# Twelve tiles' queries of a linear-attention layer, projected at the ends of the recurrent layers

## The chip, the cores and the metric

The kernel runs on one core of one Trainium2 chip. The metric is the device time of one execution, in microseconds (us).

## The reference

Four layers work in turn on x, 2048 rows of 512 bf16 numbers: a recurrent memory layer A, a linear-attention layer B, then A and B again with the same weights. Each adds its result to its input.

```python
def _B_ref(x, wqkv, wo):                       # 32 heads of 16
    qkv = (x @ wqkv).reshape(B, S, 3, H, Dh).transpose(2, 0, 3, 1, 4)
    q, k, v = qkv[0], qkv[1], qkv[2]
    phi = lambda t: jnp.where(t > 0, t + 1, jnp.exp(t)) + 1e-06
    pq, pk = phi(q), phi(k)
    kv = jnp.einsum('bhsd,bhse->bhde', pk, v)  # over all rows
    z = jnp.einsum('bhsd->bhd', pk)            # over all rows
    num = jnp.einsum('bhqd,bhde->bhqe', pq, kv)
    den = jnp.einsum('bhqd,bhd->bhq', pq, z)[..., None] + 1e-06
    return (num / den).transpose(0, 2, 1, 3).reshape(B, S, D) @ wo

x = A_x
x = x + _A_ref(_layernorm(x), mem0, Wq, Wk, Wv, Wo, seg_len)
x = x + _B_ref(_layernorm(x), wqkv, wo)
x = x + _A_ref(_layernorm(x), mem0, Wq, Wk, Wv, Wo, seg_len)
x = x + _B_ref(_layernorm(x), wqkv, wo)
```

`_A_ref` goes through 64 segments of 32 rows in order. In each, 8 memory rows and the segment's 32 rows are projected to queries, keys and values of 32 heads of 128, attend to each other under a mask, and go through Wo. The first 8 output rows are the next segment's memory, so the segments form a recurrence; the other 32 are the layer's output.

Layer B needs the sums kv and z over all rows before any output. Its queries are needed only then.

## The kernel before, in words

**Tiles and layers.** The rows form 16 tiles of 128 (four segments each). The program has two passes, called layers 0 and 1 here, each made of an A and a B. `a_layer` walks over the 64 segments s: keys and queries (`kq0`, `kq1`), values (`v`), memory attention (`mem0`, `mem1`), output projection (`out`), the next memory (`next`), the attention of the segment's own rows (`x`), and the residual (`res`). All weights of A stay in SBUF.

**The linear layer inside the recurrent one.** When a tile's four segments are done, `residual` brings their rows from `y_sb` into `dx_sb` with small DMAs, half of them from POOL's queue and half from SP's, and adds them to the tile in `x_sb` (line 2421). Then `b_in` (step `bi`) runs for the tile: layernorm (line 2058 begins it), a transposing DMA to `xlnT`, and the projection by `wqkv_sb` to keys, values and queries. Here `rows` issues, for each of four chunks of the contraction, four matmuls for the keys (line 2516) and, with the same stationary operand, four each for values and queries (line 2010). `phi` is one exponential on ACT (2489) and two DVE operations (2490, 2491). Keys and values are added to kv and z (lines 2547, 2549). The finished queries go to `pq_scratch` in DRAM and the rows of x to `xs_scratch`.

**The end of a layer.** The last tile cannot be hidden: its last segment's output, the residual, the layernorm (transposed on TensorE here, line 2075), projection, kv and z, then `b_mid` (`bm`), which folds kv and wo into one matrix `MB_sb`, follow each other. Only then can `b_out` produce a tile's output. Of layer 0, `b_out` of tiles 0 and 1 stands in this end (`bo`), because layer 1's first segments need them; the other tiles' follow in layer 1, one tile every four segments, each reading x and queries back from DRAM. Of layer 1, `b_out` of all 16 tiles (`bl`) runs at the very end, from queries and rows that `last_rows` loads four tiles at a time into the room of Wq and Wk.

**Fillers.** `spin` multiplies the constant `one_sb` with itself into a bank that nobody reads. `SPIN` lists six: one at the start of the program (`(0, 4)`), four at the end of layer 0 (`(0, 0)`, `(0, 2)`, `(0, 3)`, `(1, 1)`) and one at the end of layer 1 (`(1, 0)`).

**Order.** Every operation has a key (layer, step, name, number). The table `PLACE` gives each a due time and, for some, the engine (`a` for ACT, `v` for DVE). `schedule` sorts all operations by it, so each engine's order, DMA queues included, is written out by hand; each engine then runs its list strictly in that order and waits on semaphores. PSUM banks are given out in the same order. The due times set the order alone, nothing starts or waits by the clock.

## Time and profile before

| | us |
|---|---|
| three runs: median (lowest to highest) | 1599.27 (1597.75 to 1600.19) |
| profiled execution, own time | 1588.73 |
| its span, first to last instruction | 1586.8 |
| TensorE busy | 1522.3 (96%) |
| VectorE busy | 1218.4 (77%) |
| ScalarE busy | 986.6 (62%) |

The profile is of one execution. PE is TensorE's matmuls, PEld its weight loads, which overlap them, DVE is VectorE, ACT ScalarE, POOL GpSimd, SP the engine that only issues DMAs. A matmul's busy time includes its drain, so that consecutive ones overlap; how long one takes in a row is read from the distance of the starts. In rows of stretches the columns are the stretch, its length, busy time and count of each engine, the granted TensorE clock, the busy share of the DMA engines, and GB/s. Layer 0 ends and layer 1 begins at about 770 to 791 us; layer 1's end begins at about 1549 us.

### The profile page before, as it was taken

The page shows a single profiled execution, that of the slowest core. Times are in us where ns is not written, and L with a number is a line of the kernel's source. Part 1 is how long each engine was busy: PE and PEld are TensorE (multiplying, and loading weights), DVE is VectorE, ACT ScalarE, POOL GpSimd, SP SyncE. Part 2 cuts the span into 40 slices and gives each one's busy share as a digit, 9 for nine tenths or more (in the row PEclk, how much of TensorE's full clock was granted, in tenths as well). Part 3 has the DMA queues.
Part 4 walks back from the last instruction along what each step waited for, and adds up shares of the span by engine and source line. Part 5 has one row for each costly group of instructions (what it writes and reads, how often), then busy time and mean ns, then how long its engine had stood idle before and what let it go on. Part 6 is the DMA issues. An engine that isn't in the chain of part 4 may idle for free.

```text
span 1586.8 us, 97637 instructions
## 1 busy us (share of the span) xinstructions
PE 1522.3 (96%) x48853; PEld 820.6 (52%) x40499; DVE 1218.4 (77%) x3496; ACT 986.6 (62%) x3075; POOL 191.6 (12%) x388
## 2 busy tenths in 40 slices
PE   6999999999999999999899999999999999999997
PEld 1455555555555555555445555545555555555453
DVE  2678878877777888777688787778787778787877
ACT  2566575666666666666366666656666666666555
POOL 2011111011111101111101111011110111110110
PEclk9999999999999999999999999999999999999999
DMA  9300000001010001101000100110101110000115
GB/s 381 115 23 21 20 22 15 20 23 24 23 20 20 18 22 20 27 17 24 25 8 17 27 25 19 27 26 17 30 14 26 27 24 24 24 18 25 31 33 146
DMA packets 79347, 58.13 MB, mean 37 GB/s; under 512 B 58872, under 2 KB 73624, under 8 KB 77400
## 3 DMA queue, kind: packets, MB, share of 16 engines
q1 hardware_dynamic: 65912, 36.30, 8.7%
q0 software_dynamic: 12864, 15.46, 3.4%
q8 instruction: 350, 5.73, 1.5%
q14 instruction: 61, 0.50, 0.1%
q10 hardware_dynamic: 160, 0.14, 0.0%
HBM read 25.57 MB, written 10.35 MB: 23 GB/s over the span
## 4 chain that ended last, share of the span: by engine, by line
PE 82%; DVE 7%; ACT 5%; SPq 3%; DMA 3%; issue 1%; DVEq 0%
PE pb L2121 29%; PE pb L2010 21%; PE pb L2350 18%; PE pb L2022 8%; SPq L1924 2%; DMA dx_sb<-y_sb 2%; ACT arena_sb L1893 2%; PE pb L2516 2%; PE pb L2212 1%; PE pb L2289 1%; DVE arena_sb L1894 1%; DVE arena_sb L2141 1%; PE pb L2377 1%; DVE st_sb L2058 1%; DVE y_sb L2360 1%
## 5 line engine op out<-in xcount | busy, mean ns | idle before, releaser
L1893 ACT ACTIVATE arena_sb<-pb 128x512 bf16<-128x512 f32 (+5 forms) x1205 | 529.5, 475 | 310.9 <-PE pb L2010 174.7
L2121 PE MATMUL pb<-Wk_sb,arena_sb 128*32 128x512 bf16 x4096 | 362.6, 380 | 2.5 <-ACT arena_sb L1893 2.2
L1894 DVE CAST arena_sb<-pb 128x512 bf16<-128x512 f32 (+4 forms) x570 | 296.9, 529 | 76.8 <-PE pb L2010 46.5
L2350 PE MATMUL pb<-Wo_sb,arena_sb 128*32 128x256 bf16 x10368 | 337.6, 273 | 6.9 <-issue 2.4
L2141 DVE STREAM_TRANSPOSE arena_sb<-arena_sb 128x256 f32<-128x256 f32 x640 | 263.7, 431 | 62.0 <-ACT arena_sb L1893 55.0
L2350 PEld LDWEIGHTS pb<-Wo_sb,arena_sb 128*32 128x32 bf16 x10368 | 258.6, 96 | 48.7 <-DVE arena_sb L2260 12.5
L2022 PE MATMUL pb<-arena_sb 128*32 128x128 bf16 (+2 forms) x10800 | 270.7, 208 | 7.8 <-DVE arena_sb L1894 2.7
L2121 PE MATMUL pb<-Wq_sb,arena_sb 128*32 128x512 bf16 x3072 | 265.5, 379 | 1.1 <-ACT arena_sb L1893 0.7
L1909 POOL DMA_DIRECT2D dx_sb<-y_sb x252 | 128.2, 512 | 1135.0 <-DVE y_sb L2360 608.2
L2022 PEld LDWEIGHTS pb<-arena_sb 128*32 128x32 bf16 x10800 | 190.9, 96 | 133.6 <-issue 33.7
L2121 PE MATMUL pb<-Wv_sb,arena_sb 128*32 128x512 bf16 x2560 | 252.3, 379 | 1.3 <-DMA Wv_sb<-in_A_Wv_dram 0.9
L2010 PE MATMUL pb<-Wv_sb,arena_sb 128*32 128x512 bf16 x2560 | 252.8, 379 | 0.0
L2121 PEld LDWEIGHTS pb<-Wk_sb,arena_sb 128*32 128x32 bf16 x4096 | 109.8, 97 | 191.9 <-issue 104.4
L2010 PE MATMUL pb<-Wq_sb,arena_sb 128*32 128x512 bf16 x2048 | 200.6, 379 | 0.0
L2121 PEld LDWEIGHTS pb<-Wq_sb,arena_sb 128*32 128x32 bf16 x3072 | 84.9, 96 | 99.0 <-issue 47.1
L1893 ACT ACTIVATE outW_sb<-pb 64x256 f32<-64x256 f32 x138 | 52.2, 378 | 107.4 <-PE pb L2350 88.4
L2360 DVE TENSOR_TENSOR y_sb<-pb,outW_sb 64x256 bf16<-64x256 f32 x162 | 68.7, 424 | 57.6 <-ACT outW_sb L1893 53.7
L2260 DVE TENSOR_TENSOR arena_sb<-pb,arena_sb 128x128 bf16<-128x128 f32 x252 | 73.0, 290 | 46.6 <-PE pb L2022 16.5
L2300 DVE TENSOR_TENSOR arena_sb<-arena_sb,bo_sb 128x512 bf16<-128x512 bf16 x256 | 103.2, 417 | 2.6
L2010 PE MATMUL pb<-Wk_sb,arena_sb 128*32 128x512 bf16 x1024 | 102.1, 379 | 0.0
L2121 PEld LDWEIGHTS pb<-Wv_sb,arena_sb 128*32 128x32 bf16 x2560 | 71.0, 96 | 60.1 <-issue 34.4
L2231 ACT ACTIVATE arena_sb<-pb 128x160 bf16<-128x160 f32 x256 | 78.0, 306 | 18.9 <-PE pb L2212 11.1
(111 smaller groups left out, 1805.0 us busy)
## 6 DMA issues: line engine op xcount, KB each, us to landing
Wk_sb<-in_A_Wk_dram SPq DMA_DIRECT2D x1, 4096.0 KB, 13.7
Wq_sb<-in_A_Wq_dram SPq DMA_DIRECT2D x1, 4096.0 KB, 24.5
Wv_sb<-in_A_Wv_dram SPq DMA_DIRECT2D x1, 4096.0 KB, 34.1
Wo_sb<-in_A_Wo_dram SPq DMA_DIRECT2D x16, 256.0 KB, 7.4
xs_scratch<-x_sb POOLq DMA_DIRECT2D x32, 128.0 KB, 2.0
pq_scratch<-arena_sb POOLq DMA_DIRECT2D x31, 128.0 KB, 2.3
x_sb<-xs_scratch POOLq DMA_DIRECT2D x16, 128.0 KB, 2.5
dx_sb<-y_sb SPq DMA_DIRECT2D x126, 12.0 KB
```

The source lines that it names most:

```text
L1893: return e.activation(o() if callable(o) else o, i() if callable(i) else i, ACTF.Copy)
L1894: return e.tensor_copy(o() if callable(o) else o, i() if callable(i) else i)
L1909: add(eng, lambda e: e.dma_start(o, i), 0.55 if eng == "pool" else 0.66, reads=reads, writes=writes, dsem="%s%d" % (kind, k), lat=lat + (0 ...
L2010: return pe.add_instruction(mybir.InstMatmult(name=nc.get_next_instruction_name(), engine=mybir.EngineType.PE, ins=[pe.lower_ap(x), pe.low ...
L2022: r = pe.matmul(o[q], w[:, q], x, start=start, stop=stop, skip_group_check=True, tile_position=(0, 32 * j))
L2121: r = pe.matmul(o, blk[:, c, :], w, start=(c == 0), stop=(c == 3), tile_position=(0, 32 * j))
L2141: add("dve", lambda v: v.transpose(dst, src(img[:, k, :].bitcast(F32))), 0.445, reads=[("img", k, h) for h in range(2)], writes=[dkey])
L2231: add("act", lambda a: a.activation(PQ[:, r2, b, 64:224], tl.f32()[:, 64:224], ACTF.Exp, scale=SCALE), c_act(160), tiles=[tl], writes=[("P ...
L2260: add("dve", lambda v: v.tensor_tensor(oTb[:, s % NO, 16 * b:16 * b + 16, 0:8].rearrange("p (i j) q -> p j i q", i=4), heads(pv.f32()[:, 0 ...
L2300: add("dve", lambda v, b=b: v.tensor_tensor(Pbx[:, :, b, :].rearrange("p j (k x) -> p j k x", k=4), px[:, b, :].rearrange("p (k x) -> p k ...
L2350: r = pe.matmul(tl.f32()[32 * j:32 * j + 32, 0:256], oT[:, 4 * hh + n, :], Wo_sb[:, 8 * n + hh, 256 * d:256 * d + 256], start=(hh == 0 and ...
L2360: add("dve", lambda e: e.tensor_tensor(y_sb[0:64, k, :], tl.f32()[a, 0:256], outW[c, v, :], ALU.add), c_dve(256), reads=[("outW", w)], til ...
```

## The change

For eight tiles of layer 0 (`LATE[0]`: 8 to 13, 6 and 7) and four of layer 1 (4 to 7), `b_in` projects keys and values alone and writes the normalised rows (`xln2`) to a new DRAM scratch, `xn_scratch`, in place of the queries.

- `late_queries`, after layer 0's segments: four transposing DMAs on SP's queue bring two tiles each into buffers of layer 0 that are no longer read (`vleft[:, 0]`, `oTl[:, 0]`, `vimg[:, 0]`, `kT`). Each tile is projected, goes through `phi` and to `pq_scratch`, as before.
- `last_queries`, at the end of layer 1: one of the four loads of queries becomes a load of normalised rows of tiles 4 to 7 into the room of Wk (`XN`); their queries are projected, already transposed, straight into `XQ`.
- Five of the six fillers are removed; the one at the start of the program stays.
- The whole table `PLACE` is new, so the order of all operations changes.

```diff
+    xn_view = nc.dram_tensor("xn_scratch", [S, D], BF16, kind="Internal").ap().rearrange("(t p) d -> t p d", p=128)
-    SPIN = {(0, 0): (24, 256, 72), (1, 0): (12,), (1, 1): (22, 256, 84), (0, 2): (5,), (0, 3): (7,), (0, 4): (30, 512, 10)}
+    SPIN = {(0, 4): (30, 512, 10)}
+    LATE = {0: (8, 9, 10, 11, 12, 13, 6, 7), 1: (4, 5, 6, 7)}
...
+    def late_queries():
+        flat = lambda v: v.rearrange("p (c t x) -> p c t x", c=4, t=2)
+        rooms = [(flat(vleft[:, 0].rearrange("p b g d -> p (b g d)")), [("vl", 0, 0), ("vl", 0, 1)]),
+                 (flat(oTl[:, 0].rearrange("p n x -> p (n x)")), [("oTl", 0, 0), ("oTl", 0, 1)]),
+                 (flat(vimg[:, 0]), [("v", 0, 0), ("v", 0, 1)]),
+                 (flat(kT.rearrange("p h j x e -> p (h j x e)")), [("kT", 0), ("kT", 1)]),
+                 (flat(vimg[:, 1]), [("v", 1, 0), ("v", 1, 1)])]
+        late_t = LATE[0]
+        for (room, keys), n in zip(rooms, range(0, len(late_t), 2)):
+            t0 = late_t[n]
+            P.at(0, n, "lx")
+            add("sp", lambda e, room=room, t0=t0: e.dma_start_transpose(
+                room.rearrange("p c t x -> p c (t x)"), xn_view[t0:t0 + 2].rearrange("t p d -> (t p) d")), 1.8,
+                reads=[("xn", t0), ("xn", t0 + 1)], writes=keys, dsem="dlx%d" % n, lat=4.4)
+            for i in range(2):
+                P.at(0, n + i, "lq")
+                e, k, tq = room[:, :, i, :], ("lq", n + i), P.tile()
+                rows_of(e, keys, (0, tq))
+                phi(tq, e, k)
+                x_move(quarters(pq_view[t0 + i]), e, n + i, keys + [k], [("pq", t0 + i)], "dlq")
+
+    def last_queries():
+        for i in LATE[1][::4]:
+            for fc in range(4):
+                P.at(1, i + fc, "lq")
+                tq = P.tile()
+                for c in range(4):
+                    add("pe", lambda pe, c=c, fc=fc, i=i, tq=tq: tiled(
+                        pe, tq.f32()[:, :], wqkv_sb[:, c, 128 * fc:128 * fc + 128], XN(i)[:, c, :], c == 0, c == 3),
+                        c_pe(1, 512), reads=["wqkv", ("RE", i), ("RE", i + 1)], tiles=[tq])
+                phi(tq, XQ[:, fc, i:i + 4, :].rearrange("p t x -> p (t x)"), ("XQ", i, fc), P.res["Wq"][1])
...
     def b_in(layer, step, t):
-        if end:
+        if end or late_q:
             rows((D, tk), (2 * D, tv))
         else:
             rows((D, tk), (2 * D, tv), (0, tq))
...
+        if late_q:
+            P.count = 22
+            x_move(xn_view[t], xln2[:, ln, :], t % 4, [("xln", ln)], [("xn", t)], "dxn")
+            return
...
     def last_rows(step):
+                if not w and i in LATE[1]:
+                    nd = add("sp", lambda e, i=i: e.dma_start_transpose(XN(i), xn_view[i:i + 4].rearrange("t p d -> (t p) d")), 2.6,
+                             reads=[("xn", t) for t in range(i, i + 4)], writes=[("RE", i), ("RE", i + 1)], after=P.res["Wk"][1],
+                             dsem="dlxn%d" % i, lat=4.8)
...
     load_wo_b(1)
     a_layer(0)
+    late_queries()
     b_mid(0, NSEG + 2)
...
     last_rows(NSEG)
+    last_queries()
     b_mid(1, NSEG + 2)
```

`rows_of` is the former inner function `rows` of `b_in` with the stationary rows as an argument. The projection of a late tile loads its stationary operand by itself, where before the queries used the one that the keys had loaded.

## The prediction

> **What bounds the kernel now.** I read the page first, then four long stretches of the span, then TensorE's order of time through the end of the first layer, then the chain of waits there, and last the one place where the clock falls.

> ```profile
> span 1586.8 us, 97637 instructions
> PE 1522.3 (96%) x48853; PEld 820.6 (52%) x40499; DVE 1218.4 (77%) x3496; ACT 986.6 (62%) x3075; POOL 191.6 (12%) x388
> ```

> TensorE (PE) is busy 96% of the span. The stretches, with PE, weight loads, VectorE (DVE), ScalarE (ACT) and POOL in us, say where the rest lies:

> ```profile
> 40.00:766.00 726.00, 712.08 (x23108) 387.14 (x19156) 566.69 (x1663) 460.79 (x1456) 87.16 (x167) 1.00 0.11 26
> 766.00:791.00 25.00, 19.94 (x608) 11.46 (x528) 16.76 (x41) 8.41 (x20) 3.69 (x7) 1.00 0.09 26
> 791.00:1530.00 739.00, 720.73 (x23332) 391.62 (x19360) 580.47 (x1667) 475.71 (x1501) 86.01 (x165) 1.00 0.10 23
> 1530.00:1587.00 57.00, 45.71 (x1396) 24.84 (x1240) 42.88 (x95) 32.34 (x70) 3.67 (x7) 1.00 0.44 115
> ```

> Inside the layers PE is busy 712.08 of 726 us (98.1%) and 720.73 of 739 us (97.5%), while DVE stands near 78%. A matmul taken out there shortens the run by nearly its slot. At the ends of the layers it is different: from 766 to 791 us PE has 5.06 us idle, and part of what counts as busy is filler, the rows that write a tile from the constant `one_sb` at lines 2037 and 2010:

> ```profile
> 771.89 0.40 PE L2022 MATMUL pb<-y_sb,selz_sb 128*32 128x256 bf16 x8 [0.98 <-DVE y_sb L2360]
> 772.12 2.25 PE L2037 MATMUL pb<-one_sb 128*32 128x256 bf16 x76
> 774.19 0.72 PE L2010 MATMUL pb<-one_sb 128*32 128x256 bf16 x20
> 776.15 0.41 PE L2075 MATMUL pb<-id_sb,arena_sb 128*32 128x128 bf16 x16 [1.24 <-DVE arena_sb L2064]
> 777.09 0.40 PE L2516 MATMUL pb<-arena_sb 128*32 128x512 bf16 x4 [0.53 <-DVE arena_sb L1894]
> ...
> 778.83 0.39 PE L2516 MATMUL pb<-arena_sb 128*32 128x512 bf16 x4
> 780.75 0.24 PE L2539 MATMUL pb<-arena_sb,one_sb 128*32 128x128 bf16 x4 [1.53 <-DVE arena_sb L2491]
> ...
> 781.68 0.40 PE L2037 MATMUL pb<-one_sb 128*32 128x512 bf16 x4
> 781.89 1.04 PE L2010 MATMUL pb<-one_sb 128*32 128x512 bf16 x16
> ...
> 784.21 0.39 PE L2037 MATMUL pb<-one_sb 128*32 128x512 bf16 x4
> 784.42 1.47 PE L2010 MATMUL pb<-one_sb 128*32 128x512 bf16 x24
> 785.72 1.46 PE L2022 MATMUL pb<-arena_sb 128*32 128x128 bf16 x32
> 787.00 2.58 PE L2037 MATMUL pb<-one_sb 128*32 128x256 bf16 x88
> 789.49 0.61 PE L2022 MATMUL pb<-arena_sb 128*32 128x512 bf16 x8
> 790.69 0.83 PE L2121 MATMUL pb<-Wq_sb,arena_sb 128*32 128x512 bf16 x12
> ```

> From first start to the next work the four fillers take about 2.6 us (772.12 on), 1.1 (781.68 to 782.75), 1.5 (784.21 to 785.72) and 2.5 (787.00 to 789.49): 7.7 us. With the 5.06 us idle, some 12.7 us of PE are free in this end. What sets its length is a chain that goes through DVE, ACT and one DMA:

> ```profile
> 768.72 0.43 SPq L1909
> 769.19 3.64 DMA dx_sb<-y_sb
> 772.93 0.43 DVE x_sb L2421
> ```

> **What is taken out of the layers.** A tile's query projection is four groups of four matmuls with 512 columns. Eight such groups start between 777.09 and 778.83 us, so one takes 1.74 / 8 = 0.2175 us and a tile 0.87 us. Eight tiles of layer 0 and four of layer 1 make 7.0 + 3.5 = 10.4 us. Since 2% of these stretches is PE waiting for others, and these waits need not shrink, I take off a tenth, 1.0 us (bounds 0 and 2). That leaves 9.4 us. The queries' ACT and DVE work also leaves; these engines have slack there, so that gains nothing by itself. On POOL the write of the normalised rows takes the place of the write of the finished queries, 128 KB each, in each of the twelve tiles; the eight writes of layer 0's late queries come later, behind the chain.

> **What is added at the end of layer 0.** 7.0 us of matmuls against 12.7 us free: by capacity they fit. The changed order puts a first tile's groups into the last segments and 52 query matmuls (13 groups, 2.8 us) between the row pick and the layernorm's turns, where the first filler and its idle time filled 772.12 to 776.15. I cost them on PE at nothing; without that cover they would cost up to 7.0 us. Each tile brings one exponential on ACT and two operations on DVE:

> ```profile
> L2491 DVE SCALAR_TENSOR_TENSOR arena_sb<-pb,arena_sb 128x512 bf16<-128x512 f32 x64 | 43.2, 680 | 0.8
> L2489 ACT ACTIVATE arena_sb<-pb 128x512 bf16<-128x512 f32 x64 | 36.6, 593 | 21.3 <-PE pb L2010 18.3 <-PE pb L2022 1.9 <-PE pb L2532 1.1
> L2490 DVE TENSOR_SCALAR arena_sb<-arena_sb 128x512 bf16<-128x512 bf16 x64 | 18.1, 284 | 14.7 <-ACT arena_sb L2489 14.2
> ```

> DVE gets 8 x (0.680 + 0.284) = 7.7 us where it has 25 - 16.76 = 8.2 us free, and the chain runs through DVE. A chain step that arrives behind a 0.68 us operation waits for it. Against that, 3.64 us of the chain is a DMA, during which DVE has little else to do, and a late query may spill into the next layer's first segments, since its tile is read much later. Bounds 0 and 7.7 us; I take 1.5, nearer the low end because ACT has over 16 us free and DVE's free time just holds the work.

> **The end of layer 1.** The four tiles' matmuls (3.5 us) replace this filler, 2.6 us long:

> ```profile
> 1551.95 0.39 PE L2037 MATMUL pb<-one_sb 128*32 128x512 bf16 x4
> 1552.17 2.54 PE L2010 MATMUL pb<-one_sb 128*32 128x512 bf16 x44
> ```

> Their 4 x 0.964 = 3.9 us on DVE meet 57 - 42.88 = 14.1 us free, but behind 1562 us that engine is nearly full. Bounds 0 and 3.9 us; I take 0.7.

> **The added transposing loads.** Layer 0's end gets four loads of two tiles on SP's queue, and one of layer 1's four loads takes normalised rows in place of queries.

> ```profile
> L2049 SPq DMA_TRANSPOSE arena_sb<-pq_scratch x16: 1197/1200/2328, 714.3 to 1445.3; - x16
> L2618 SPq DMA_TRANSPOSE Wq_sb<-pq_scratch x4: 1757/1956/2857, 1540.7 to 1554.0; - x4
> arena_sb<-pq_scratch SPq DMA_TRANSPOSE x16, 2.8
> Wq_sb<-pq_scratch SPq DMA_TRANSPOSE x4, 4.7
> ```

> A load of one tile holds the queue 1.20 us and lands in 2.8, of four tiles 1.96 and 4.7; one of two tiles I estimate at 1.45 and 3.4 us. In the changed order three of them stand directly ahead of the layer's last moves of `dx_sb`, the DMA of the chain above. Two wait for TensorE's last reads of a value buffer and of the keys, so the moves are queued behind these waits, and the DVE addition of line 2421 behind the moves. Bounds: 0, and 3 x 1.45 = 4.4 us. I take 0.4, since the last rows are written after the keys' last use, and the loads should be issued by then.

> **The fillers' clock.** Without fillers PE is less dense, and this kernel shows what that can do:

> ```profile
> 1044.70:1048.10 3.40, 0.83 (x24) 0.33 (x16) 1.56 (x5) 0.22 (x2) 0.56 (x1) 1.00 0.00 0
> 1048.00:1050.00 2.00, 1.45 (x35) 0.46 (x30) 2.00 (x7) 1.31 (x6) 0.00 (x0) 0.54 0.18 66
> 1050.00:1052.00 2.00, 1.72 (x68) 1.10 (x57) 1.11 (x4) 1.32 (x6) 0.00 (x0) 0.61 0.63 127
> 1559.80:1563.20 3.40, 1.48 (x60) 0.99 (x64) 3.11 (x11) 1.52 (x3) 0.00 (x0) 1.00 1.06 346
> PE pb L2220 <- DVE arena_sb L2141: 4.3, 4, 3.0
> 1042.92 0.52 POOL L1909 DMA_DIRECT2D dx_sb<-y_sb  x1 [2.85 <-DVE st_sb L2059]
> DVE x_sb L2421 <- DMA dx_sb<-y_sb: 13.2, 16, 3.4
> ```

> After 3.40 us with 0.83 us of work (24%) the granted clock fell to 0.54 and 0.61; with 1.48 us (44%) it stayed at 1.00. If the third and fourth filler of layer 0 went and nothing took their place, the 3.4 us before 789.49 would hold the work of 786.1 to 787.0, 0.9 us (26%), which is close to the first. A fall costs about half of 3.4 us, 1.7. Bounds 0 and 1.7; I take 0.5. [...]

> **The stall at 1046 us.** The same rows show a loss that the change does not aim at. A move of `dx_sb` from POOL started only at 1042.92, after 2.85 us, DVE stood 3.4 us at line 2421, PE 3.0 us, and then the clock fell for about 3.4 us: 3.0 us and at least 1 us in slower matmuls, some 4 us. It hangs on what DVE runs between the row sum and line 2421, and the whole order is made anew, so it may vanish (4.0 us gained), stay or come up elsewhere (0). One bad case in about 31 such places here says that one such stall is as likely as none: I take half, 2.0. [...]

> **The sum.** -10.4 + 1.0 + 1.5 + 0.7 + 0.4 + 0.5 = -6.3, and -2.0 for the stall: -8.3 us. The profiled execution took 1588.73 us (span 1586.8), so it would be 1580.4. The runs' median is 1599.27, 10.5 us above it; nothing in the trace says where these lie, so I carry the difference over unchanged: 1599.3 - 8.3 = 1591.0 us.

> **The rivals.** (a) DVE becomes the bound of the ends. Its place is 769 to 791 and 1550 to 1562 us, its price all of the 7.7 + 3.9 = 11.6 us on the chain, with the clock and SP at 1.7 and 0.4: -9.4 + 11.6 + 2.1 = +4.3, 1603.6 us. It ends slower once more than 7.3 of the 11.6 us land on the chain. For it: the chain there is DVE's. Against: 8.2 and 14.1 us free, and spilling is allowed. (b) The stall stays and the new order adds one more of 4 us: -6.3 + 4.0 = -2.3, 1597.0 us. For it: 16 waits at line 2421 show how tight these moves are; against: 15 of them sum to 9.8 us. (c) The move does not shorten the layers: each segment's memory feeds the next, and if that recurrence were the bound, the removed groups would turn into waits: 0 + 1.5 + 0.7 - 2.0, about 1599.5 us. PE's 98% speaks against it.

> **How the numbers follow.** The forecast gets 0.72, (a) 0.10, (b) 0.12, (c) 0.06. The forecast's own range is 1587.0 (stall gone, ends 2 us less than taken) to 1595.0 (stall kept, 2 us more on the ends). To hold 8 in 10 the whole range takes in (b) and the edge of (c): 1586.5 to 1599.5. Faster by over 0.2% (3.2 us, about what a measurement of this kernel can tell from no change): 0.72 and a part of (b), 0.77. Within: the rest of (b) and (c), 0.13. Slower: (a), 0.10.

> **What would show it.** Right: the last layernorm of layer 0 (line 2058's counterpart, 774.17 us before) some 6 us earlier, the first key products of layer 1 (790.69) 4 to 6 us earlier, no rows on `one_sb` at these ends, query groups in their place, PE still at 98% inside. Wrong: PE waiting in the ends for DVE in pieces of 0.7 us; a PE wait for `xn_scratch`; a long wait at line 2421; a clock below 1.00 near 790 us.

## The result, and the profile after

| | us |
|---|---|
| changed kernel, median of 9 runs (lowest to highest) | 1591.70 (1586.66 to 1594.18) |
| kernel before on the same chip, 9 runs | 1597.77 (1594.76 to 1601.56) |
| ratio, 95% interval | 0.9955 [0.994, 0.997] |
| profiled execution after, own time / span | 1591.70 / 1589.9 |

Faster by 0.45%, some 7 us (4.8 to 9.6). The forecast was 1591.0. In these and the later sets the kernel before had medians of 1594.9 to 1597.8, under the 1599.27 of the three runs that the prediction started from: the time came out right, the gain was forecast a little too large. The changed kernel was timed in one set alone. Four later kernels that differ from it by small edits (a_nodve, a_fill, a_act, a_fill_act, below) were 2.4 to 5.7 us under the kernel before of their own sets, so the 7 us may be on the high side. The first lines of the page after, and four stretches of it (stretch, length, PE, weight loads, DVE, ACT and POOL busy, granted clock, DMA share, GB/s):

```profile
span 1589.9 us, 97342 instructions
PE 1517.8 (95%) x48573; PEld 822.2 (52%) x40515; DVE 1222.8 (77%) x3529; ACT 985.0 (62%) x3042; POOL 198.1 (12%) x396
```

```profile
40.00:766.00 726.00, 707.28 (x22988) 386.83 (x19160) 559.33 (x1638) 459.71 (x1456) 87.43 (x167) 1.00 0.12 27
766.00:792.00 26.00, 20.08 (x500) 10.33 (x472) 21.93 (x55) 13.54 (x29) 7.51 (x12) 0.91 0.29 50
792.00:1530.00 738.00, 716.96 (x23176) 391.64 (x19272) 581.94 (x1695) 465.95 (x1452) 87.84 (x168) 1.00 0.11 23
1530.00:1590.00 60.00, 50.20 (x1504) 27.95 (x1380) 46.82 (x107) 36.80 (x79) 4.22 (x8) 0.99 0.46 114
```

PE is still at 97% inside the layers. At the end of layer 0 DVE went from 16.76 of 25 us to 21.93 of 26, and the granted clock from 1.00 to 0.91. TensorE's order of time there (start, duration, operation, and the idle time before it with what ended it):

```profile
772.43 0.40 PE L2034 MATMUL pb<-y_sb,selz_sb 128*32 128x256 bf16 x8 [0.63 <-DVE y_sb L2373]
772.66 2.98 PE L2519 MATMUL pb<-arena_sb 128*32 128x512 bf16 x52
775.59 0.41 PE L2088 MATMUL pb<-id_sb,arena_sb 128*32 128x128 bf16 x16
...
785.16 1.49 PE L2034 MATMUL pb<-arena_sb 128*32 128x128 bf16 x32 [1.74 <-DMA arena_sb<-pq_scratch]
789.28 1.05 PE L2034 MATMUL pb<-arena_sb 128*32 128x512 bf16 x8 [2.64 <-DVE arena_sb L2723]
790.11 0.65 PE L2088 MATMUL pb<-id_sb,arena_sb 128*32 128x128 bf16 x16
790.54 1.07 PE L2034 MATMUL pb<-arena_sb 128*32 128x512 bf16 x8
791.39 1.93 PE L2134 MATMUL pb<-Wq_sb,arena_sb 128*32 128x512 bf16 x16
```

The 52 query matmuls stand where the first filler stood and take 2.98 us, about the 2.8 that the prediction gave them. The other two gaps are bare now: 1.74 us for the transposing load of tile 1's queries, 2.64 us for DVE. Behind them the sixteen matmuls of `Wq_sb` take 1.71 us to the next start at 793.10, 0.107 us each, twice the 0.2175 / 4 of the prediction: the granted clock is 0.50. Four stretches around it:

```profile
783.70:787.10 3.40, 1.45 (x32) 0.59 (x32) 2.66 (x8) 2.58 (x5) 0.00 (x0) 1.00 0.08 20
787.10:790.50 3.40, 1.22 (x24) 0.66 (x28) 3.31 (x8) 1.19 (x4) 0.00 (x0) 0.50 0.00 0
790.50:793.90 3.40, 3.40 (x44) 0.97 (x28) 1.95 (x4) 0.42 (x2) 1.51 (x2) 0.50 0.54 111
794.00:798.00 4.00, 4.00 (x80) 0.97 (x40) 2.31 (x6) 1.56 (x5) 0.50 (x1) 1.00 0.08 4
```

**A yardstick for all runs.** In the table below, the first matmul of each "next memory" (line 2377 before, 2390 after) cuts the span: layer 0 runs from that of segment 0 to that of segment 62, its end from there to segment 0 of layer 1, and so on. The columns of waits need a word. One of the page's DMA queues has about one packet for every 256 instructions of TensorE, and I take it to bring TensorE's program in pieces:

```profile
q8 instruction: 350, 5.73, 1.5%
```

350 packets of 16,384 bytes for 89,788 instructions of TensorE recorded in before (matmuls, weight loads and 436 that only wait): about 256 instructions a piece. In dense stretches, above all in the output products (line 2350 before, 2363 after), TensorE halts without any wait that the profile knows ("issue"), and in all fourteen profiles each such halt stands at one place modulo 256 of its instruction stream (193 or 194, counted from the first recorded instruction). I call that place a boundary. After a boundary the next packet starts a median of about 1 us later, and where TensorE halts at the following boundary it goes on a median of 2.5 to 2.6 us after that packet's start. "Waits" sums, over all boundaries, the longest distance of two starts next to the boundary less 0.10 us, where it is over 0.22 us; w0 and w1 are the parts of it in layers 0 and 1.

```
kernel         layer 0     w0  end 0  layer 1     w1  end 1     span  waits  span-waits
before           708.6    2.3   48.8    730.4    2.8   49.6   1586.8    5.5      1581.3
b_again          713.2    3.4   47.7    735.5    6.3   49.6   1595.3   10.1      1585.2
b_pad            720.9   11.1   47.3    745.1   18.0   50.5   1613.2   29.2      1584.0
b_nospin         713.9    4.3   51.2    741.3   13.8   51.8   1607.7   19.0      1588.7
b_noq            714.5    8.3   47.8    735.0   11.0   51.1   1597.9   21.1      1576.8
b_thin           710.2    4.8   47.9    727.3    4.3   51.5   1586.3    9.5      1576.8
b_thin_nophi     711.2    4.3   47.7    727.4    6.1   50.3   1586.1   10.8      1575.3
after            708.8    5.4   50.0    731.4    3.9   50.4   1589.9   10.2      1579.7
a_nodve          706.0    7.7   49.3    733.5    6.5   52.4   1590.8   14.9      1575.9
a_fill           710.4    8.6   47.9    732.3    5.2   50.1   1590.0   14.6      1575.4
a_act            707.4    7.6   50.2    732.2    4.6   51.5   1590.8   12.9      1577.9
a_fill_act       706.2    6.0   47.8    734.3    4.4   51.1   1588.8   10.7      1578.1
a_pad            721.2   20.9   50.3    743.9   17.6   53.1   1618.0   41.0      1577.0
a_wide           714.6   10.5   50.7    740.6   14.4   51.9   1607.2   27.2      1580.0
```

Each line is one profile. Two of the same kernel (before, b_again) differ by 8.5 us in the span and by 3.9 us less the waits; smaller differences of single profiles are not read.

### The profile page after: what moved, and what is told of

Same layout as the page of the kernel before. It is cut to its first block, busy times and chain, and to the rows that moved or that the text cites. A ratio compares the mean times of both kernels' runs of the same rounds, so it can differ in the third digit from the quotient of the medians.

```text
span 1589.9 us, 97342 instructions
## 1 busy us (share of the span) xinstructions
PE 1517.8 (95%) x48573; PEld 822.2 (52%) x40515; DVE 1222.8 (77%) x3529; ACT 985.0 (62%) x3042; POOL 198.1 (12%) x396
## 4 chain that ended last, share of the span: by engine, by line
PE 80%; DVE 7%; ACT 4%; DMA 3%; SPq 3%; issue 1%; POOL 0%; DVEq 0%
PE pb L2134 29%; PE pb L2022 20%; PE pb L2363 17%; PE pb L2034 8%; DMA dx_sb<-y_sb 3%; SPq L1936 2%; PE pb L2519 2%; ACT arena_sb L1904 2%; PE pb L2225 1%; DVE arena_sb L1905 1%; PE pb L2302 1%; PE pb L2390 1%; DVE y_sb L2373 1%; DVE arena_sb L2154 1%; DVE st_sb L2071 1%
## 5 line engine op out<-in xcount | busy, mean ns | idle before, releaser
L1905 DVE CAST arena_sb<-pb 128x512 bf16<-128x512 f32 (+4 forms) x586 | 301.1, 522 | 84.8 <-PE pb L2022 40.3
L2034 PE MATMUL pb<-arena_sb 128*32 128x128 bf16 (+1 forms) x10800 | 278.3, 208 | 12.4 <-DVE arena_sb L2723 3.0
L2363 PEld LDWEIGHTS pb<-Wo_sb,arena_sb 128*32 128x32 bf16 x10368 | 260.0, 96 | 46.7 <-DVE arena_sb L2273 11.9
L2022 PE MATMUL pb<-Wv_sb,arena_sb 128*32 128x512 bf16 x2560 | 252.9, 378 | 0.0
L2022 PE MATMUL pb<-Wq_sb,arena_sb 128*32 128x512 bf16 x2048 | 201.8, 380 | 0.0
L2022 PE MATMUL pb<-Wk_sb,arena_sb 128*32 128x512 bf16 x1024 | 101.9, 380 | 0.0
```

Of the source, the lines that this page charges most:

```text
L1905: return e.tensor_copy(o() if callable(o) else o, i() if callable(i) else i)
L2022: return pe.add_instruction(mybir.InstMatmult(name=nc.get_next_instruction_name(), engine=mybir.EngineType.PE, ins=[pe.lower_ap(x), pe.low ...
L2034: r = pe.matmul(o[q], w[:, q], x, start=start, stop=stop, skip_group_check=True, tile_position=(0, 32 * j))
L2363: r = pe.matmul(tl.f32()[32 * j:32 * j + 32, 0:256], oT[:, 4 * hh + n, :], Wo_sb[:, 8 * n + hh, 256 * d:256 * d + 256], start=(hh == 0 and ...
```

## The experiments

**b_again**, the kernel before once more, with no edit.

> The kernel before, unchanged, for a second profile of it: the first one's own time, 1588.73 us, lies below all nine of its timed runs (1594.76 to 1601.56). If the time of a run hangs on how often the row moves to dx_sb come late, this profile, nearer to 1598 us, shows some 8 to 10 us more of DVE waiting at line 2421 and of PE idle inside the layers. If instead a profile is simply shorter than a timed run, it shows about 1589 us and the same waits as the first.

1597.0 us, span 1595.3. The first profile of before was an untypically short execution; a profile is not simply shorter than a timed run. VectorE's waits ahead of line 2421 are 17.7 us against 13.2, some 4.5 more, half of what the first theory asked for. The stall at 1046 us on which the prediction built is in this profile too, at 1052 us. POOL waits as long before its last move, VectorE stands nearly as long (here the profile puts it down to "issue"), and TensorE's longest wait is 2.8 us:

```profile
POOL dx_sb L1909 <- DVE st_sb L2059: 2.8, 1, 2.8
DVE x_sb L2421 <- issue: 3.3, 1, 3.3
PE pb L2220 <- DVE arena_sb L2141: 6.8, 8, 2.8
```

Only the fall of the clock is not there. POOL's wait stands at this place in all seven profiles of before's order (b_pad, b_nospin, b_noq, b_thin and b_thin_nophi below are the others) and in none of the changed order. Segment 20 of layer 1, which holds it, takes 15.4 us in before, 14.2 in b_again, 12.4 to 13.6 in the other five, and 11.3 to 11.9 in the changed order.

**b_noq**, before without the twelve tiles' queries:

```diff
-        if end:
+        late_q = t in {0: (8, 9, 10, 11, 12, 13, 6, 7), 1: (4, 5, 6, 7)}[layer]
+        if end or late_q:
             rows((D, tk), (2 * D, tv))
...
-        phi(tq, eq_sb, "eq")
+        if late_q:
+            P.count += 3
+        else:
+            phi(tq, eq_sb, "eq")
```

> The kernel before without the query projection and the phi of the twelve late tiles in their old place (48 groups of four matmuls, 12 exponentials, 24 DVE operations); their stale queries are still written, so the DMAs stay. Leaves out part of the computation: those tiles' outputs use the queries of an earlier tile. Prediction's step: -9.4 us against before (bounds -8.4 and -10.4), about 1588.4 us. Rival (c), the segments' recurrence is the bound: 0 to -2 us.

1602.41 us (1597.98 to 1607.01), ratio 1.0033 [1.0018, 1.0049]: slower, with less to do. The page of waits shows where (TensorE, line, releaser: total, times, longest), b_again first:

```profile
PE pb L2350 <- issue: 3.3, 8, 0.8
```

```profile
PE pb L2350 <- issue: 8.3, 19, 1.2
```

In the table its waits are 21.1 us against 10.1, and less the waits it is 8.4 us shorter than b_again. Taking instructions out moves everything behind them against the pieces of 256.

**b_nospin**, before without five of its six fillers (`SPIN = {(0, 4): (30, 512, 10)}`).

> The kernel before without the five fillers at the layers' ends; nothing else changes. Prediction's step: +0.5 us (0 to +1.7): the clock falls once near 787 to 790 us, PE's rows after it take twice their slot for 3.4 us. Rival: the fillers hold up the chain, and their removal gains 0.5 to 2 us.

1609.54 us (1608.11 to 1611.96), ratio 1.0081 [1.0062, 1.01], a miss by 12 us. The clock stood at half for 17.0 us in all near 779, 793 and 1574 us, the two ends grew by 3.5 and 2.2 us, and the waits for instructions by 8.9: two effects in one edit, so that it priced neither alone.

**a_nodve**, the changed kernel without the two VectorE operations of `phi` for the late tiles.

> The changed kernel without the two DVE operations of the late tiles' phi (their queries are the bare exponentials, so those tiles' outputs differ). Prediction's step: the late queries' DVE work costs 1.5 + 0.7 us on the chains, so 2.2 us less than the changed kernel, about 1589.5 us. Rival (a), DVE is the bound of the ends: 5 to 11 us less, 1587 to 1580 us. If the chains wait for loads and for PE instead: no change.

1592.47 us (1587.67 to 1594.82), ratio 0.997 [0.9958, 0.9982], no gain on the changed kernel's 0.9955. The sixteen operations at the end of layer 0 and the eight in layer 1's cost nothing on the chain that can be measured in the time; in the one profile the end of layer 0 is 0.7 us shorter than in the changed kernel's.

**b_pad and a_pad** ask of the pieces alone: 128 instructions more in the start filler, ahead of all work, at about the same time.

```diff
-(0, 4): (30, 512, 10)}
+(0, 4): (56, 256, 34)}
```

> The kernel before with the start filler of TensorE made of 224 matmuls of 256 columns and 38 of them with their own weight load, in place of 120 of 512 columns and 14: 128 instructions more, about the same time, ahead of all work. Every later instruction keeps its order but stands half a piece of 256 further on. Theory 1: within 1 us of before. Theory 2: the waits for instructions inside the output products fall elsewhere; the run moves by 2 to 8 us, in either direction, and the sum of these waits (10.1 us in the second profile of before) by as much.

> The changed kernel with the same start filler of 128 more instructions. Theory 1: within 1 us of the changed kernel (1591.7). Theory 2: 2 to 8 us away from it in either direction, by as much as the waits for instructions change (10.2 us in its profile).

b_pad 1614.6 us (1612.72 to 1617.0), ratio 1.0113 [1.0099, 1.0128]; a_pad 1616.52 (1611.75 to 1619.8), ratio 1.0122 [1.0104, 1.0141]. So half a piece costs before 18 us and the changed kernel some 27 (1.67% of 1596), more than either side had put down; the order of every later instruction is the same. In b_pad the waits went up by 19.1 us, the whole loss; in a_pad by 30.8. The waits on instructions of b_pad and then a_pad:

```profile
PE pb L2350 <- issue: 10.5, 22, 1.0
PE pb L2022 <- issue: 4.6, 9, 0.8
PE pb L2121 <- issue: 2.3, 4, 0.9
```

```profile
PE pb L2363 <- issue: 19.9, 29, 1.7
PE pb L2034 <- issue: 4.6, 12, 0.8
```

One of them in a_pad, in the order of time:

```profile
290.12 0.21 PE L2022 MATMUL pb<-arena_sb,bo_sb 128*32 128x64 bf16 x4
290.45 0.62 PE L2363 MATMUL pb<-Wo_sb,arena_sb 128*32 128x256 bf16 x15
291.94 0.62 PE L2363 MATMUL pb<-Wo_sb,arena_sb 128*32 128x256 bf16 x16 [0.86 <-issue]
```

The products run on in a row until 290.80, and the next starts at 291.94 for no other engine's sake; it stands at the boundary, and the last packet on the instruction queue had started at 289.17, 2.8 us earlier. Of the two offsets tried, before and the changed kernel both stand at the better one (5.5 to 10.2 us of waits), so the pieces are not what made the change faster; by the table they are what made b_noq slower. In the fourteen profiles the waits at boundaries came to 5.5 to 41.0 us of a run.

**b_thin** takes only the work out and leaves each instruction:

```diff
+                        n = 64 if late_q and i == 2 else D
...
-    r = again(pe, dst.f32()[q, :], xlnT[:, c, q], wqkv_sb[:, c, o:o + D],
+    r = again(pe, dst.f32()[q, 0:n], xlnT[:, c, q], wqkv_sb[:, c, o:o + n],
```

> The kernel before, with the query matmuls of the twelve tiles (eight of layer 0, four of layer 1) cut from 512 to 64 columns and everything else left in place: every instruction stays, only TensorE time goes. It leaves out seven eighths of these tiles' queries. Theory 1 (the layers are bound by TensorE, a matmul taken out shortens the run by nearly its slot): 48 groups x 0.2175 us x 7/8 = 9.1 us, a tenth off: 8.2 us faster than before, ratio 0.995. Theory 2 (leaving the instructions out cost time because the stream of TensorE's instructions is fetched in pieces of 256 and every piece boundary moved): the boundaries stay, so most of the 8 us comes, 5 to 8 us, where the kernel without these queries gained nothing. Theory 3 (a segment's recurrence is the bound, not TensorE): 0 to 1 us.

1593.7 us (1588.03 to 1595.09), ratio 0.9978 [0.9967, 0.9989]: 3.5 us, between the theories. The waits stayed (9.5 us).

**b_thin_nophi**, the same without `phi` for these tiles.

> The kernel before with the twelve tiles' query matmuls cut to 64 columns, and also without the exponential and the two VectorE operations that make the queries positive (these tiles' queries are left out, stale ones are written). TensorE's instructions all stay. Theory A (VectorE shares the bound inside the layers, so that TensorE's work alone gives only a part): 12 x 4 x 0.964 us = 46 us of VectorE work go too, and the run gains 3 to 5 us on the kernel with narrow matmuls alone (1593.7), to about 1590. Theory B (VectorE has slack, what was missing went into waits that are the order's own): within 1.5 us of 1593.7.

1587.83 us (1584.02 to 1592.16), ratio 0.9958 [0.9942, 0.9973]: 6.7 us, some 3 more than b_thin. That speaks for theory A, though the two intervals overlap; the VectorE work that went is 12 x 0.964 = 11.6 us, the expectation's factor of 4 is a slip. Its profile is shorter by only 0.2 us than b_thin's, so this stays a reading of the times.

**a_wide** puts the twelve tiles' matmuls back into the changed kernel's layers:

```diff
-        if end or late_q:
+        if late_q:
+            rows((D, tk), (2 * D, tv), (0, tv))
+        elif end:
             rows((D, tk), (2 * D, tv))
```

> The changed kernel with the twelve tiles' 512-column query matmuls put back beside those of keys and values, on TensorE alone: they are added into the values' accumulator (these tiles' values are therefore other sums), nothing else runs more. The late queries at the ends stay. So it is the same TensorE work inside the layers as before the change. Theory 1 (TensorE is the bound inside the layers): 48 x 0.2175 = 10.4 us, less a tenth: 9.4 us slower than the changed kernel, about 1601. Theory 3 (half of it goes into waits of the recurrence, as the kernel with narrow matmuls showed): 3.5 to 5 us slower, about 1596.

1612.08 us (1608.93 to 1617.15), ratio 1.0112 [1.0095, 1.0129], far beyond both theories. Its 192 added matmuls moved the pieces: waits 27.2 us against 10.2, which is all of the 17.3 us between the two spans. Less the waits it is 1580.0, a little above the changed order's 1575.4 to 1579.7; its layer 0 is 3.5 us longer than the mean of the other six (704.1 against 700.6), its layer 1 no longer (726.2 against 727.6). As a price of the matmuls it failed; for that each instruction would have had to stay, as in b_thin.

**a_fill**, two fillers back at the end of layer 0, exactly 256 instructions (28 + 28 and 100 + 100 matmuls and weight loads):

```diff
-    SPIN = {(0, 4): (30, 512, 10)}
+    SPIN = {(0, 3): (7, 512, 24), (1, 1): (25, 256, 96), (0, 4): (30, 512, 10)}
```

> The changed kernel with two fillers put back at the end of layer 0, 28 matmuls of 512 columns and 100 of 256 with a weight load each: 256 instructions in all, so that the later pieces of 256 begin where they did. Theory of the clock (the two waits of 1.74 and 2.64 us before layer 1 halved the clock for 6.8 us, 787.1 to 793.9): no stretch at half clock near 790 us, 2 to 3.4 us faster than the changed kernel, about 1589. Rival (the end is set by its chain, TensorE at half clock has time): no stretch at half clock, but within 1 us of 1591.7.

1591.02 us (1586.05 to 1593.45), ratio 0.9964 [0.995, 0.9977]. In the profile the clock stays up and the end takes 47.9 us in place of 50.0:

```profile
783.70:787.10 3.40, 3.36 (x80) 1.47 (x72) 2.89 (x8) 2.54 (x5) 0.00 (x0) 1.00 0.61 77
787.10:790.50 3.40, 3.16 (x100) 2.69 (x104) 3.10 (x8) 1.99 (x4) 0.00 (x0) 1.00 0.02 5
790.50:793.90 3.40, 3.40 (x92) 1.63 (x73) 3.33 (x7) 1.11 (x4) 1.50 (x2) 1.00 0.22 41
```

So the theory of the clock holds for the stretch (2.1 us), but the run as a whole is no faster than the changed kernel: 14.6 us of waits against 10.2 in the one profile, and an interval of 4 us, hide it. In this profile the clock also fell for 3.4 us at 1381 us, inside segment 48 of layer 1, where the changed kernel's did not.

**a_act.** In layer 1 the changed kernel's segment 48 takes 13.5 us where b_again's takes 11.2 (a_nodve 13.1, a_fill 14.8; b_thin 11.2). VectorE and POOL there, in the changed kernel:

```profile
1373.49 0.43 DVE L2373 TENSOR_TENSOR y_sb<-pb,outW_sb 64x256 bf16<-64x256 f32 x1 [0.23 <-ACT outW_sb L1904]
...
1378.62 0.42 DVE L2434 TENSOR_TENSOR x_sb<-x_sb,dx_sb 128x512 bf16<-128x512 bf16 x1 [2.47 <-DMA dx_sb<-y_sb]
```

```profile
1371.83 1.08 POOL L1921 DMA_DIRECT2D dx_sb<-y_sb  x2 [8.77 <-DVE y_sb L2373]
1374.26 1.51 POOL L1921 DMA_DIRECT2D dx_sb<-y_sb  x3 [1.36 <-issue]
```

```diff
-    ("dy", "dz")[d], ("pool", "sp")[d])
+    ("da", "dz")[d] if (layer, G) == (1, 11) else ("dy", "dz")[d],
+    ("act", "sp")[d] if (layer, G) == (1, 11) else ("pool", "sp")[d])
```

> The changed kernel, where in layer 1 the five moves of half rows of tile 11 that POOL issues go out from ScalarE's queue instead. In four profiles of the changed order, and in none of before, POOL stood 1.36 us between two of them, VectorE then waited 2.1 to 2.5 us for their data at line 2434, and segment 48 of layer 1 took 2 to 3.5 us longer. Theory (this stall is on the path): it goes, 2 to 3 us faster than the changed kernel, about 1589. Rival (the data come late because the last output rows come late): VectorE waits as long, within 1 us of 1591.7.

1593.43 us (1590.79 to 1594.05), ratio 0.9985 [0.9973, 0.9996], and the wait is still there:

```profile
1373.42 0.43 DVE L2373 TENSOR_TENSOR y_sb<-pb,outW_sb 64x256 bf16<-64x256 f32 x1
...
1378.71 0.42 DVE L2435 TENSOR_TENSOR x_sb<-x_sb,dx_sb 128x512 bf16<-128x512 bf16 x1 [2.62 <-DMA dx_sb<-y_sb]
```

This does not clear POOL by itself, because ScalarE's queue issues its last moves between 1374.71 and 1376.26 us, no earlier than POOL did. But in a_pad and a_wide POOL halts for 1.36 us at the same place, while VectorE waits 0.90 and 0.48 us and segment 48 takes 11.9 and 11.8 us: the halt alone does not make the wait (and the expectation's four profiles are three). The last output rows come at 1373.9 us and their sum is due at 1376.1, whichever queue carries one half. Whether SP's half, which stayed, or the order behind it holds it was not tried.

**a_fill_act**, both mends together.

> Both mends together: the two fillers of 256 instructions at the end of layer 0, which kept the clock at full speed and took that end from 50.0 to 47.9 us, and the five moves of tile 11 from ScalarE's queue. If both hold and instruction waits stay near 10 us: 2.0 + 2 to 3 us under the changed kernel, 1587 to 1588. If the fillers' gain goes into more instruction waits again (14.4 us against 10.0): 1590.

1590.13 us (1585.83 to 1590.83), ratio 0.9965 [0.9952, 0.9979]. Neither expected value was hit clearly, and its interval holds the changed kernel's ratio: no version was found that is shown to beat the changed kernel.

## Why the prediction was right, and where only by luck

**The layers' removal (-10.4 + 1.0 = -9.4).** The sum came close, but not in the places and not shown to come from the removed matmuls. Less the waits for instructions (layer 0 less w0) layer 0 takes 706.3, 709.8 and 709.8 us in before, b_again and b_pad (mean 708.6), and 698.3 to 703.4, mean 700.6, in the six kernels of the changed order (all but a_wide): -8.0, where eight tiles were to give 7.0 less a tenth. Layer 1 takes 727.6, 729.2 and 727.1 (728.0) before, and 726.3 to 729.9 (727.6) in the changed order: -0.4, where 3.5 less a tenth was forecast. In before's order, without these queries, it is the other way round: b_noq, b_thin and b_thin_nophi gave 1.7 to 3.2 us in layer 0 and 4.0 to 6.7 in layer 1 (721.3 to 724.0).

So the new order seems to have a part in the 8.0 us. Putting the matmuls back (a_wide) cost 3.5 of them in one profile; the rest goes with the queries' VectorE and ScalarE work or with the order, and no run has the new order with all queries in their old place. In layer 1 the stall that went (2.7 us in segment 20) and the new one (2.1 in segment 48) nearly cancel, and where the matmuls' 3 us stayed is open.

Two steps of the prediction did not stand. That a matmul taken out shortens the run by nearly its slot: 9.1 us of slots gave 3.5 us in b_thin. And that the queries' ACT and DVE work in the layers gains nothing by itself: b_thin_nophi speaks for some 3 us, though its interval does not settle it.

**The end of layer 0 (+1.5 DVE, +0.4 SP, +0.5 clock).** The sum, 2.4, is close to what came: 49.9 us in the mean of after, a_nodve, a_act and a_pad against 47.9 before, 2.0. Its terms were wrong. DVE on the chain was mis-sized, 1.5 where a_nodve's end is 0.7 shorter in one profile and its time no better. SP's 0.4 is not seen: VectorE's last wait for `dx_sb` there is 0.87 us, against 1.09 before. The clock was mis-sized the other way: 0.5 where a_fill shows 2.1 (a_fill_act 2.2). The step that failed is the bound of 1.7 us: it took one stretch of 3.4 us, and there were two, 6.8 us in all; the first of them was itself only 36% busy (1.22 of 3.40). The stretch ahead of it was 43% busy (1.45), next to the 44% that the prediction had read as safe at 1560 us. That stretch was cut at the wrong place: the falls of one profile lie a whole number of 3.41-us steps apart (in the changed kernel's those at 49.84 and 787.11 us, 216 steps), and on the steps of before's fall at 1048.2 us the stretch from 1560.17 us is 50% busy. The prediction had the two places, as fillers of 1.5 and 2.5 us, but not what holds TensorE at the first, the wait for tile 1's load. It lands 4.4 us after its issue, where the prediction's rows had 2.8, while three writes to `pq_scratch` are under way; whether they hold it was not tried:

```profile
pq_scratch<-arena_sb POOLq DMA_DIRECT2D x3, 128.0 KB, 3.8
arena_sb<-pq_scratch SPq DMA_TRANSPOSE x1, 4.4
```

**The end of layer 1 (+0.7).** 50.4 us in the changed kernel, 51.4 in the mean of its six kernels, against 49.9: 0.5 to 1.5. The prediction has no clock term here, and the clock fell in this end for 3.4 us in a_nodve, a_act and a_fill_act. It fell there in b_noq, b_thin and b_thin_nophi too, whose filler was in place.

**The stall at 1046 us (-2.0).** Right in kind. It stands in every profile of before's order and in none of the changed order, and less the waits for instructions segment 20 is 2.7 us shorter there; only the fall of the clock, counted in the 4 us, belonged to one execution. The 2.0 was half of 4 by a guess, so its nearness is luck. VectorE's waits for `dx_sb` as a whole hardly changed (b_again 14.4 us and the 3.3 above):

```profile
DVE x_sb L2434 <- DMA dx_sb<-y_sb: 14.4, 13, 2.5
```

Of rival (b) the half came true: a stall came up in a new place (segment 48), at about half its price of 4 us, but the old one did not stay.

**The starting point.** The forecast took the median of three runs, 1599.27, and left the 10.5 us to the profile's own time unexplained. b_again shows that the profile was short: 1.5 us too high a start and a gain put 1 to 2 us too high nearly cancelled. What the prediction said one would see came partly: no `one_sb` rows and queries in their place, as said; but the last layernorm of layer 0 began at 773.61 us against 774.17, not 6 us earlier, and layer 1's first projection at 791.39 against 790.69. Beside b_again (777.50 and 794.00) they are 3.9 and 2.6 us earlier, where some 6 and 4 to 6 were forecast; the half clock's 2.1 us lies between the two. By stretches the forecast was -6.3, +2.4, -5.1 (the stall with it) and +0.7 us for layer 0, its end, layer 1 and its end; the table gives -8.0, +2.0, -0.4 and +0.5 to +1.5. Layer 1 is the largest miss, and that the time came out at 1591.7 is in part luck.

**The rivals.** (a), VectorE as the bound of the ends, falls with a_nodve. (c), that the layers would give nothing because the segments' recurrence is the bound, is not what b_thin shows, 3.5 us of 9.1; layer 1 of the changed order looks like it (-0.4 us), for a reason that stays open.

## What to carry to other kernels

Take work out of a stream, for a test, by making instructions smaller and not fewer: b_thin kept the pieces where they were and could be read, b_noq and a_wide could not. In a program of tens of thousands of TensorE instructions look at the "issue" waits in the densest line first; a shift of 128 instructions by a filler was worth 18 to 27 us here, more than the change itself. And take two profiles of the kernel before, and look for a stall in both under every name: the one of the prediction stood in the second too, but as "issue", and its clock fall did not.

## What the runs showed of the hardware

In the fourteen profiles the clock fell to half 18 times between the start and the last few us. Each time TensorE had been busy 23 to 56% of the 3.4 us ahead; a stretch of 44% (a_pad) and several of 50% were not followed by a fall, so about half is all that can be said. The half clock lasted 6.8 us where the next 3.4 us were 34 to 56% busy, and 3.4 us where they were 79 to 100% busy.
